# High halves of v and z by casting transfers of GpSimd, the half key tile as two 64-row products, and the logits of two half tiles in one pass

## The chip, the core and the metric

The program runs on one core of a Trainium2 chip. Time is the device time of one execution in microseconds (us). Five engines work side by side, each through its own list of instructions in order: TensorE (PE: matmul; PEld: the loading of its weights), VectorE (DVE), ScalarE (ACT), GpSimd (POOL), and SyncE (SP), which here only issues transfers between the chip's memory and the core. A granted clock of 1.00 in the profile is TensorE at 2.4 GHz.

## The reference, cut to what matters

Attention without a softmax over eight batches, and then a mixture of experts whose input is the attention's output.

```python
# u, v: (8, 2496, 256); z: (8, 2496, 64)
scores = scale * np.matmul(z, z.transpose(0, 2, 1))      # scale = 1 / 2496
attn = np.maximum(scores, 0.0) ** 2
x = u * np.matmul(attn, v)
logits = x @ w_gate                                       # (19968, 8)
# tokens are handed out to 8 experts, best logit first, 2496 to each
out[mask] = np.maximum(x[mask] @ w1[e], 0.0) @ w2[e]      # for each expert e
```

## The kernel before

A product in full precision is made of three in TensorE's faster number format (F32R): an operand a is split into a high part h = a rounded to that format and a low part l = a - h, and a.b is h.h + h.l + l.h. Most of the work beside TensorE is this splitting: a copy with a cast makes h, a subtraction makes l.

**Tiles.** A batch has 2496 tokens: 19 key tiles of 128 and a half one of 64, so KT = 20 with NT = 19 the number of the half one. Queries come in NQ = 5 groups, four of 512 columns and group 4 of 448. The program walks `seq`, 8 x 5 x 20 = 800 steps (b, g, kt). In step n, `av(n)` multiplies v's key tile kt with the squared scores r of that tile and adds to two accumulators acc0 and acc1 (the two halves of the 256 columns of v). A whole key tile takes six products of 128 rows.

**The half key tile.** v's 64 rows and z's 64 columns stand twice in their tiles, in rows 0 to 63 and 64 to 127. In r both halves are the same then. `split_lo` puts the low part into rows 64 to 127 of the high tile itself, so that one product of 128 rows gives h + l; `av` needs only four products (lines 1006 and 1009, for d = 0 and 1).

**Scores.** z has 64 channels, so score products have 64 rows; they stand in pairs, one on rows 0 to 63 and one on 64 to 127. `scores` makes 20 key tiles (GO = KT) in one burst of 60 products, at the start of each group, right behind the half key tile of the last group: it makes the key tiles 4 to 19 of the group that begins and 0 to 3 of the next. `rectify` takes them from one of six buffers (SCB) by ScalarE, and numbers 3, 6, 9 and 12 of a burst by VectorE (ASIDE).

**Splitting.** `square` (ScalarE), `split_hi` and `split_lo` (VectorE, line 993) run LA = 4 steps ahead of `av`, with five buffers of each. `split_hi` is ScalarE's (line 982) but for every second tile of group 4 (line 984, VectorE). z and v of batch b are loaded and split during group 4 of batch b - 1: `split_v` at step n0 - 20 + kt, `split_z` every fourth step (n0 is the batch's first step): on ScalarE for the high part (lines 935 and 943), on VectorE for the low part (936, 944). v's tiles turn in a ring of 22 buffers.

**The rest of VectorE.** At the end of a group it transposes the accumulators (`turn_acc`, line 1015) and multiplies with u (`times_u`, 1021); SP writes x out and reads it back as XS with tokens in partitions (`put_x`), and `post_logits` (line 1045) makes one column of logits of one tile: 32 passes for each group, 8 of them in group 4 on a tile of 64 rows. `logits_at` says at which steps they stand: `own` of them in the next group, `go` right behind the burst after that, `late` in the steps that follow it.

From step 20 on the program's order is the order on PE, ACT and DVE (`manual_schedule`); GpSimd and SP take their transfers in an order that the scheduler makes. Lines 748, 652 to 654, 590 and 781 belong to the expert part, which starts behind attention at about 1375 us; lines 590 and 781 are GpSimd's indirect gathers and scatters.

## Time and profile before

| | |
|---|---|
| time before, median of 3 runs | 2465.4 us (2464.53 to 2467.0) |
| the profiled execution, its own time | 2466.28 us |
| its span, first to last instruction | 2464.5 us |
| mean granted clock of TensorE | 0.996 |
| busy: PE, DVE, ACT, POOL | 98%, 84%, 62%, 15% of the span |
| largest groups of instructions: PE lines 1006, 1009, 1008 | 621.0, 615.9, 586.8 us |

A row of the timeline has the start in us, the time taken in us, engine, line, operation, the tile written and the tiles read, partitions x elements, the count, and in brackets the idle time of the engine before it with what ended it. Products are pipelined: one that "takes" 0.39 is followed by the next 0.23 later, so the pace is read from the starts. Instructions of one form that follow each other are merged into a row.

### The profile page before, as it was taken

To read this page: it belongs to the slowest core of one execution; us is meant where nothing else is said; L and a number is where in the kernel's file an instruction comes from. 1 tells how busy PE (TensorE), PEld (TensorE's weight loads), DVE (VectorE), ACT (ScalarE), POOL (GpSimd) and SP (SyncE) were. 2 spreads that over 40 slices of the span, in tenths; PEclk is the share of its full clock that TensorE was granted. 3 is DMA by queue.
4 is the path that set the end of the run, shared out by engine and by line. 5 is a ranking of instruction groups with operands and counts; after the bars stand their busy time and mean duration, and the time that the engine had idled before them with its cause. 6 is when DMAs were issued, how large, how long until landed. Compare 5 with 4: busy or idle time off the path is not lost.

```text
span 2464.5 us, 42329 instructions
## 1 busy us (share of the span) xinstructions
PE 2416.7 (98%) x14948; PEld 2016.6 (82%) x14948; DVE 2067.0 (84%) x6309; ACT 1535.1 (62%) x2986; POOL 362.5 (15%) x508
## 2 busy tenths in 40 slices
PE   8999999999999999999999899999999999999997
PEld 6888888888888888888887787788888888888886
DVE  7899898998999998989989897879796969696332
ACT  7898888898898988888987123333333333343332
POOL 3000000000000000000000022233242433333332
PEclk9999999999999999999999999999999999999999
DMA  4132131131131321312211022121212111122111
GB/s 150 34 105 62 52 114 30 53 110 52 45 109 37 100 66 52 114 27 55 76 52 43 9 70 69 34 73 47 70 51 69 44 64 54 45 86 68 43 42 34
DMA packets 156852, 154.86 MB, mean 63 GB/s; under 512 B 89440, under 2 KB 129888, under 8 KB 156512
## 3 DMA queue, kind: packets, MB, share of 16 engines
q1 hardware_dynamic: 141408, 110.72, 15.1%
q0 software_dynamic: 15232, 41.44, 5.3%
q8 instruction: 117, 1.92, 0.3%
q14 instruction: 95, 0.78, 0.1%
HBM read 111.22 MB, written 40.89 MB: 62 GB/s over the span
## 4 chain that ended last, share of the span: by engine, by line
PE 86%; DVE 8%; issue 3%; ACT 1%; DMA 1%; POOL 1%; POOLq 0%; ACTq 0%; DVEq 0%; SPq 0%
PE acc L1006 14%; PE acc L1009 14%; PE acc L1008 13%; PE sc L961 10%; PE y L748 10%; PE hp L652 5%; PE hp L653 5%; PE y L750 5%; PE hp L654 5%; PE srch L281 1%; DVE lo L993 1%; PE srch L529 1%; DVE vl L944 1%; DVE mask L124 1%; DVE lt L1045 1%
## 5 line engine op out<-in xcount | busy, mean ns | idle before, releaser
L1006 PE MATMUL acc<-hi,vh 128*128 128x512 f32 (+1 forms) x1600 | 621.0, 388 | 2.8 <-DVE hi L984 2.7
L1009 PE MATMUL acc<-hi,vl 128*128 128x512 f32 (+1 forms) x1600 | 615.9, 385 | 0.0
L1008 PE MATMUL acc<-lo,vh 128*128 128x512 f32 (+1 forms) x1520 | 586.8, 386 | 0.2 <-DVE lo L993 0.2
L993 DVE TENSOR_TENSOR lo<-r,hi 128x512 fp32r<-128x512 f32 (+1 forms) x760 | 510.5, 674 | 55.9 <-ACT hi L982 50.2
L730 ACT ACTIVATE hh<-hp 128x512 fp32r<-128x512 f32 (+1 forms) x319 | 187.2, 587 | 592.1 <-PE hp L654 474.1
L982 ACT ACTIVATE hi<-r 128x512 fp32r<-128x512 f32 (+1 forms) x701 | 454.3, 648 | 112.6 <-ACT r L977 65.0
L977 ACT ACTIVATE r<-r 128x512 f32<-128x512 f32 (+1 forms) x800 | 505.5, 643 | 2.7 <-DVE r L971 2.5
L1045 DVE SCALAR_TENSOR_TENSOR lt<-xs,wgb 128x256 bf16<-128x256 f32 x1248 | 473.4, 419 | 1.9
L748 PE MATMUL y<-w,hh 128*128 128x512 f32 x1216 | 447.7, 400 | 2.2 <-DVE y L773 1.4
L1006 PEld LDWEIGHTS acc<-hi,vh 128*128 128x128 f32 x1600 | 300.8, 188 | 72.9 <-issue 14.5
L973 ACT ACTIVATE r<-sc 128x512 f32<-128x512 f32 (+1 forms) x638 | 314.0, 614 | 53.5 <-PE sc L961 52.5
L1009 PEld LDWEIGHTS acc<-hi,vl 128*128 128x128 f32 x1600 | 300.8, 188 | 55.1 <-DVE vl L944 0.2
L1008 PEld LDWEIGHTS acc<-lo,vh 128*128 128x128 f32 x1520 | 285.8, 188 | 56.0 <-DVE lo L993 5.0
L748 PEld LDWEIGHTS y<-w,hh 128*128 128x128 f32 x1216 | 228.3, 188 | 51.7 <-DVE y L773 2.6
L652 PE MATMUL hp<-xh,w1h 128*128 128x512 f32 (+2 forms) x642 | 256.7, 400 | 2.1 <-DVE hl__30375 L732 1.3
L590 POOL DMA_INDIRECT xg<-xd,idx x160 | 176.7, 1104 | 540.4 <-issue 244.7
L961 PE MATMUL sc<-z,z 64*128 64x512 f32 (+1 forms) x1920 | 243.6, 393 | 8.9 <-DVE r L971 5.8
L653 PE MATMUL hp<-xl,w1h 128*128 128x512 f32 (+2 forms) x642 | 251.1, 391 | 0.1
L654 PE MATMUL hp<-xh,w1l 128*128 128x512 f32 (+2 forms) x642 | 249.0, 388 | 0.0
L961 PEld LDWEIGHTS sc<-z,z 64*128 64x128 f32 x1920 | 197.3, 185 | 48.5 <-issue 11.7
L256 POOL IOTA slot<- 128x256 bf16 x1 | 1.5, 1531 | 1346.4 <-DVE nrem L366 1346.4
L781 POOL DMA_INDIRECT out_dram<-y,idx x160 | 163.5, 1022 | 195.8 <-DVE y L773 111.6
(1180 smaller groups left out, 3173.6 us busy)
## 6 DMA issues: line engine op xcount, KB each, us to landing
ur<-in_u_dram SPq DMA_DIRECT2D x39, 512.0 KB, 3.9
vr<-in_v_dram SPq DMA_DIRECT2D x32, 512.0 KB, 3.9
xd<-tr SPq DMA_DIRECT2D x128, 128.0 KB, 2.3
xs<-xd SPq DMA_DIRECT2D x32, 512.0 KB, 4.5
wr<-in_moe_w_dram SPq DMA_DIRECT2D x32, 512.0 KB, 4.9
zr<-in_z_dram SPq DMA_DIRECT2D x40, 256.0 KB, 3.0
xd<-tr SPq DMA_DIRECT2D x28, 112.0 KB, 2.1
vr<-in_v_dram SPq DMA_DIRECT2D x8, 384.0 KB, 3.4
```

What stands on the lines that cost most here:

```text
L652: nc.tensor.matmul(p[:, c], wh, xh, start=(d == 0), stop=False)
L653: nc.tensor.matmul(p[:, c], wh, xl, start=False, stop=False)
L654: latest["mm"] = nc.tensor.matmul(p[:, c], wl, xh, start=False, stop=(d == DH - 1))
L748: nc.tensor.matmul(o, h[:, c], w.rearrange("p s d -> p (s d)"), start=(f == 0), stop=(f == FT - 1), skip_group_check=True)
L961: nc.tensor.matmul(pair[s], key[b, p][r, c * 128:c * 128 + 128], query[b, g][r, :w], start=key is ZH and query is ZH, stop=key is ZL)
L977: nc.scalar.activation(R[n], R[n], AF.Square)
L982: nc.scalar.activation(h, R[n], AF.Copy)
L993: recent["l"] = nc.vector.tensor_sub(l, a, h.bitcast(F32))
L1006: nc.tensor.matmul(o, vh, h, start=(kt == 0), stop=False)
L1008: nc.tensor.matmul(o, vh, l, start=False, stop=False)
L1009: nc.tensor.matmul(o, vl, h, start=False, stop=last)
L1045: nc.vector.scalar_tensor_tensor(t[r], XS[b, g][r, i], 1.0, WG["rows"][r, e], op0=OP.mult, op1=OP.mult, accum_out=lg[r, j, e:e + 1])
```

## The change

- `split_z` and `split_v` for all batches but the first have no copy by ScalarE: GpSimd's queue loads the high part straight from memory, with the cast in the transfer, into the tile zh or vh. The low parts are functions of their own, `low_z` and `low_v`, four steps later; the loads of z and v that they subtract from move with them (z from m - 8 to m - 2, v from 4g - 8 to 4g - 4).
- `split_hi` is ScalarE's for every tile from step 20 on, those of group 4 too.
- For the half key tile `split_lo` writes a low tile like the others, and `av` makes three pairs of 64-row products: rows 0 to 63 for d = 0 and rows 64 to 127 for d = 1.
- The half tiles of two batches share a tile TAIL, an even batch in rows 0 to 63 and an odd one in 64 to 127; the odd one's passes make the logits of both. `logits_at` gets other numbers.

```diff
@@ def split_z, split_v
-            src = ZI.pop((b, g))
-            return (nc.scalar.activation(ZH[b, g], src, AF.Copy),
-                    nc.vector.tensor_sub(ZL[b, g], src, ZH[b, g].bitcast(F32)))
+            if b:
+                nc.gpsimd.dma_start(ZH[b, g], z[b, :, 512 * g:512 * g + 512])
+                return
+            return nc.scalar.activation(ZH[b, g], ZI[b, g], AF.Copy), low_z(b, g)
+
+        def low_z(b, g):
+            return nc.vector.tensor_sub(ZL[b, g], ZI.pop((b, g)), ZH[b, g].bitcast(F32))
 
         def split_v(b, kt):
-            src = VR[b, kt // 4][:, kt % 4]
-            h = vp.tile([128, D], F32R, name="vh")
-            l = vp.tile([128, D], F32R, name="vl")
-            with in_turn(b):
-                nc.scalar.activation(h, src, AF.Copy)
-                nc.vector.tensor_sub(l, src, h.bitcast(F32))
-            VH[b, kt], VL[b, kt] = h, l
+            VH[b, kt] = vp.tile([128, D], F32R, name="vh")
+            if b == 0:
+                with in_turn(b):
+                    nc.scalar.activation(VH[b, kt], VR[b, kt // 4][:, kt % 4], AF.Copy)
+                    low_v(b, kt)
+            elif kt < NT:
+                nc.gpsimd.dma_start(VH[b, kt], v[b, 128 * kt:128 * kt + 128])
+            else:
+                for c in range(2):
+                    nc.gpsimd.dma_start(VH[b, kt][c * TL:(c + 1) * TL], v[b, 128 * kt:])
+
+        def low_v(b, kt):
+            VL[b, kt] = vp.tile([128, D], F32R, name="vl")
+            nc.vector.tensor_sub(VL[b, kt], VR[b, kt // 4][:, kt % 4], VH[b, kt].bitcast(F32))
@@ def split_hi, split_lo
-            if n >= KT and (seq[n][1] != NQ - 1 or n % 2 or n == B * NQ * KT - 2):
+            if n >= KT:
                 nc.scalar.activation(h, R[n], AF.Copy)
...
-            if seq[n][2] == NT:
-                nc.vector.tensor_sub(h[TL:], a[TL:], h[TL:].bitcast(F32))
-                return
-            l = wk.tile([128, 512], F32R, name="lo", bufs=LA + 1)[:, :width(seq[n][1])]
-            recent["l"] = nc.vector.tensor_sub(l, a, h.bitcast(F32))
-            LO[n] = l
+            LO[n] = wk.tile([128, 512], F32R, name="lo", bufs=LA + 1)[:, :width(seq[n][1])]
+            recent["l"] = nc.vector.tensor_sub(LO[n], a, h.bitcast(F32))
@@ def av
-            last = kt == NT
-            h, l = HI.pop(n), LO.pop(n, None)
-            for d in range(2):
-                o = ACC[b, g][d][:, :width(g)]
-                c = slice(d * 128, (d + 1) * 128)
-                vh, vl = VH[b, kt][:, c], VL[b, kt][:, c]
-                nc.tensor.matmul(o, vh, h, start=(kt == 0), stop=False)
-                if not last:
-                    nc.tensor.matmul(o, vh, l, start=False, stop=False)
-                nc.tensor.matmul(o, vl, h, start=False, stop=last)
+            o = [ACC[b, g][d][:, :width(g)] for d in range(2)]
+            c = [slice(d * 128, (d + 1) * 128) for d in range(2)]
+            h, l, vh, vl = HI.pop(n), LO.pop(n), VH[b, kt], VL[b, kt]
+            parts = ((vh, h), (vh, l), (vl, h))
+            if kt < NT:
+                for d in range(2):
+                    for i, (w, x) in enumerate(parts):
+                        nc.tensor.matmul(o[d], w[:, c[d]], x, start=(kt == 0 and i == 0), stop=False)
+                return
+            for i, (w, x) in enumerate(parts):
+                for d in range(2):
+                    r = slice(d * TL, (d + 1) * TL)
+                    nc.tensor.matmul(o[d], w[r, c[d]], x[r], start=False, stop=(i == 2))
@@ def put_x, post_logits
+                if b % 2 == 0:
+                    TAIL[b // 2] = wk.tile([128, D], F32, name="tail", bufs=1)
                 r = TL * (b % 2)
-                nc.sync.dma_start(XS[b, g][r:r + TL, n], xd[lo + 128 * n:lo + w])
+                nc.sync.dma_start(TAIL[b // 2][r:r + TL], xd[lo + 128 * n:lo + w])
...
-                r = slice(TL, 128) if b % 2 else slice(0, TL)
-                j = B * NT + b // 2
+                r, src, j = slice(0, 128 if b % 2 else TL), TAIL[b // 2], B * NT + b // 2
@@ def logits_at
-            own, go, late = ((11, 12, 9), (16, 12, 4), (20, 10, 2), (0, 14, 18), (6, 14, 12))[n % NQ]
+            own, go, late = ((8, 14, 10), (14, 12, 6), (22, 10, 0), (0, 14, 18), (4, 14, 14))[g]
             if n == B * NQ - 3:
-                own, go, late = 20, 12, 0
+                own, go = 20, 12
+            if g == NQ - 1 and b % 2 == 0 and b + 2 < B:
+                own, go, late = 4, 12, 8
@@ the plan of a batch
-                    at(m - 8, load_z, b, g)
+                    at(m - 2, load_z, b, g)
                     at(m + 1, split_z, b, g)
-                    at(n0 - KT + 4 * g - 8, load_v, b, g)
+                    at(m + 5, low_z, b, g)
+                    at(n0 - KT + 4 * g - 4, load_v, b, g)
                 for kt in range(KT):
                     at(n0 - KT + kt, split_v, b, kt)
+                    at(n0 - KT + kt + 4, low_v, b, kt)
```

How the order moves, at three places. On TensorE at the end of group 1 of batch 3, where the score burst of group 2 follows; before (acc_7353 and acc_7354 are the two accumulators, z_... the z tiles):

```order
L1009 MATMUL acc_7354<-hi,vl 128x512
L1006 MATMUL acc_7353<-hi,vh 128x512
L1009 MATMUL acc_7353<-hi,vl 128x512
L1006 MATMUL acc_7354<-hi,vh 128x512
L1009 MATMUL acc_7354<-hi,vl 128x512
L961 MATMUL sc<-z_6532,z_6465 128x512 x12
```

and after:

```order
L1014 MATMUL acc_7383<-hi,vl 128x512
L1019 MATMUL acc_7382<-hi,vh 128x512
L1019 MATMUL acc_7383<-hi,vh 128x512
L1019 MATMUL acc_7382<-lo,vh 128x512
L1019 MATMUL acc_7383<-lo,vh 128x512
L1019 MATMUL acc_7382<-hi,vl 128x512
L1019 MATMUL acc_7383<-hi,vl 128x512
L972 MATMUL sc<-z_6549,z_6488 128x512 x12
```

Four products of 128 rows have become six of 64 rows, alternating between the accumulators; the score products still follow at once.

On VectorE from the last steps of group 4 of batch 2 to the first ones of batch 3, across the burst at 522.14 us (r<-sc are the four rectifications, lt the logits); before:

```order
L944 TENSOR_TENSOR vl<-vr,vh 128x256
L971 TENSOR_SCALAR r<-sc 128x512 x4
L1021 TENSOR_TENSOR tr<-tr,ur 128x512
L1021 TENSOR_TENSOR tr<-tr,ur 128x384
L1045 SCALAR_TENSOR_TENSOR lt,lg<-xs,wgb 128x256 x14
L993 TENSOR_TENSOR lo<-r,hi 128x512
L1045 SCALAR_TENSOR_TENSOR lt,lg<-xs,wgb 128x256 x2
L993 TENSOR_TENSOR lo<-r,hi 128x512
L1045 SCALAR_TENSOR_TENSOR lt,lg<-xs,wgb 128x256 x2
L993 TENSOR_TENSOR lo<-r,hi 128x512
```

and after:

```order
L956 TENSOR_TENSOR vl<-vr,vh 128x256
L982 TENSOR_SCALAR r<-sc 128x512 x4
L1031 TENSOR_TENSOR tr<-tr,ur 128x512
L1031 TENSOR_TENSOR tr<-tr,ur 128x384
L1055 SCALAR_TENSOR_TENSOR lt,lg<-xs,wgb 128x256 x14
L1001 TENSOR_TENSOR lo<-r,hi 128x512
L956 TENSOR_TENSOR vl<-vr,vh 128x256
L1055 SCALAR_TENSOR_TENSOR lt,lg<-xs,wgb 128x256 x2
L1001 TENSOR_TENSOR lo<-r,hi 128x512
L956 TENSOR_TENSOR vl<-vr,vh 128x256
L1055 SCALAR_TENSOR_TENSOR lt,lg<-xs,wgb 128x256 x2
L1001 TENSOR_TENSOR lo<-r,hi 128x512
```

The vl ahead of the rectifications is that of key tile 15 now and was that of 19; four subtractions of vl stand among the first steps of the new batch.

On GpSimd, whose list had no transfer during attention, this stands for batch 4, after the change (z_10651 is the first z tile of batch 5, one batch ahead; the next four are those of batch 4):

```order
L949 DMA vh<-in_v_dram 128x256 x2
L935 DMA z_10651<-in_z_dram 128x512
L935 DMA z_8700<-in_z_dram 128x512
L935 DMA z_8761<-in_z_dram 128x512
L935 DMA z_8828<-in_z_dram 128x512
L935 DMA z_8897<-in_z_dram 128x512
L949 DMA vh<-in_v_dram 128x256 x17
L952 DMA vh<-in_v_dram 64x256 x2
```

26 transfers for a batch have come in; the z tile of batch 1 stands ahead of them all, near the start of the program.

## Rows read from the trace of the kernel before

**Rows 1.** Waits of TensorE, 165 to 1330 us: total us, times, longest.
```profile
PE sc L961 <- DVE r L971: 5.3, 7, 0.8
```
**Rows 2.** Timeline of TensorE, end of a group and its normal burst.
```profile
590.70 0.39 PE L1009 MATMUL acc<-hi,vl 128*128 128x512 f32 x1
...
591.61 0.39 PE L1009 MATMUL acc<-hi,vl 128*128 128x512 f32 x1
591.92 1.66 PE L961 MATMUL sc<-z,z 64*128 64x512 f32 x12
...
599.18 0.50 PE L1006 MATMUL acc<-hi,vh 128*128 128x512 f32 x1
```
**Rows 3.** Timeline of TensorE, the burst at the start of batch 3.
```profile
522.14 4.08 PE L961 MATMUL sc<-z,z 64*128 64x512 f32 x30
526.97 3.79 PE L961 MATMUL sc<-z,z 64*128 64x512 f32 x30 [0.74 <-DVE r L971]
530.68 0.50 PE L1006 MATMUL acc<-hi,vh 128*128 128x512 f32 x1
```
**Rows 4.** Timeline of VectorE, ahead of and in the same burst.
```profile
519.00 0.39 DVE L984 CAST hi<-r 128x448 fp32r<-128x448 f32 x1
...
525.93 0.38 DVE L944 TENSOR_TENSOR vl<-vr,vh 128x256 fp32r<-128x256 f32 x1
526.24 1.88 DVE L971 TENSOR_SCALAR r<-sc 128x512 f32<-128x512 f32 x3
```
**Rows 5.** Timeline of VectorE, the normal burst of rows 2.
```profile
593.68 0.66 DVE L971 TENSOR_SCALAR r<-sc 128x512 f32<-128x512 f32 x1
```
**Rows 6.** Stretches, group 4: us; busy PE, PEld, DVE, ACT, POOL; clock; DMA; GB/s.
```profile
490.80:522.10 31.30, 31.30 (x179) 27.61 (x178) 30.14 (x82) 30.35 (x71) 0.00 (x0) 1.00 0.44 135
```
**Rows 7.** Waits of VectorE in that stretch, 490.8 to 522.1 us.
```profile
DVE r L971 <- PE sc L961: 0.7, 2, 0.4
```
**Rows 8.** Timeline of TensorE, products of 448 columns: batch 2, last batch.
```profile
497.60 0.47 PE L1006 MATMUL acc<-hi,vh 128*128 128x448 f32 x1
...
1357.41 0.36 PE L1006 MATMUL acc<-hi,vh 128*128 128x448 f32 x1
...
1371.40 0.36 PE L1006 MATMUL acc<-hi,vh 128*128 128x448 f32 x1
```
**Rows 9.** Groups of instructions by form: busy us, mean ns of one, idle before.
```profile
L982 ACT ACTIVATE hi<-r 128x448 fp32r<-128x448 f32 x81 | 49.0, 605 | 33.2 <-issue 24.8 <-PE acc L1009 5.4 <-ACT r L977 2.9
...
L943 ACT ACTIVATE vh<-vr 128x256 fp32r<-128x256 f32 x160 | 70.9, 447 | 0.0
```
**Rows 10.** Timeline of GpSimd, gathers one behind the other.
```profile
1733.74 0.96 POOL L590 DMA_INDIRECT xg<-xd,idx  x1 [0.30 <-issue]
1735.01 0.95 POOL L590 DMA_INDIRECT xg<-xd,idx  x1 [0.30 <-issue]
```
**Rows 11.** Timeline of GpSimd and TensorE, a gather and what waited for it.
```profile
1432.66 1.43 POOL L590 DMA_INDIRECT xg<-xd,idx  x1 [0.31 <-issue]
...
1435.97 0.44 PE L684 MATMUL y<-identf,xg 128*128 128x128 f32 x2 [0.45 <-DMA xg<-xd,idx]
```
**Rows 12.** Transfers issued: count, KB each, median us to landing.
```profile
vr<-in_v_dram SPq DMA_DIRECT2D x32, 512.0 KB, 3.9
```
**Rows 13.** Timeline of VectorE and TensorE, key tile 8 of batch 3, group 0.
```profile
540.35 0.68 DVE L993 TENSOR_TENSOR lo<-r,hi 128x512 fp32r<-128x512 f32 x1
...
541.95 0.39 PE L1008 MATMUL acc<-lo,vh 128*128 128x512 f32 x1
```
**Rows 14.** Timeline of TensorE at the start.
```profile
7.36 0.79 PE L961 MATMUL sc<-z,z 64*128 64x512 f32 x2 [1.76 <-ACT z L935]
```
**Rows 15.** Stretches at the start, columns as in rows 6.
```profile
6.00:8.00 2.00, 0.64 (x4) 0.54 (x6) 0.66 (x2) 0.63 (x1) 1.24 (x14) 1.00 1.07 359
```
**Rows 16.** Timeline of TensorE, last group of attention.
```profile
1352.26 0.47 PE L1006 MATMUL acc<-hi,vh 128*128 128x448 f32 x1 [2.68 <-DVE hi L984]
```
**Rows 17.** Timeline of VectorE at that place.
```profile
1351.82 0.39 DVE L984 CAST hi<-r 128x448 fp32r<-128x448 f32 x1
```

14 lines of the change are left out of this document (7 added, 7 removed).

## The prediction, made before the changed kernel ran

> **What bounds the kernel now.** I read the waits of TensorE first, then its timeline at the ends of the query groups, then VectorE at the same places. Between 165 and 1330 us TensorE waits for nothing but a VectorE result, 5.3 us in seven waits [rows 1]; all the rest of attention is its own issue rate. So an edit there is worth either matmul time that goes away or one of the few stalls. Three of those can be seen.
>
> First the normal end of a group: a product of 512 columns every 0.2275 us ((591.61 - 590.70)/4), a gap of 0.31 instead of that at the change to the 64-row score products, then 60 of them in 7.26 us (591.92 to 599.18) [rows 2]. They run in pairs, so a pair costs at most 7.26/30 = 0.242.
>
> Second, the score burst at the start of a batch, after group 4: 8.54 us (522.14 to 530.68) for the same 60 products, with a wait for VectorE in the middle [rows 3]. That is 1.28 more than in [rows 2], and there are seven such bursts (the seven waits of [rows 1]). The reason is in VectorE's rows: its first rectification comes 4.10 us after the burst's start (526.24), in the normal burst 1.76 after (593.68 against 591.92) [rows 2 to 5]. Had it begun at 524.96, 1.28 earlier and 2.82 after the start, TensorE would have lost nothing. It is late because group 4 of every batch but the last carries the splitting of the next batch's v and z: VectorE is busy 30.14 of 31.30 us and ScalarE 30.35 [rows 6], and VectorE waits only 0.7 us in the whole stretch [rows 7].
>
> Third, within that group TensorE takes 24.54 us (497.60 to 522.14 [rows 3, 8]) for 118 products of 448 columns. The same form without v and z beside it takes (1371.40 - 1357.41)/69 = 0.2028 each [rows 8], 23.93 for 118; with 0.2 for the way in and out some 0.4 per batch is lost to operands that come just in time.
>
> **The half key tile.** Before, four 128-row products for each group; now three pairs of 64-row products. Before: 4 x 0.2275 = 0.910. After: three pairs at 0.242 or less. The 7.26 of the burst hold its own way in and out (the first product behind it took 0.50 instead of 0.39 [rows 2]), so I take 0.235 a pair, 0.705 in all, and a gain of 0.20; the ends are 0.184 (0.242 a pair) and 0.2275 (a pair as cheap as one product). In the order the six stand right ahead of the score products, which have the same 64-row form, so the gap of 0.31 only moves from behind them to ahead of them. 32 groups x 0.20 and seven groups of 448 columns x 0.175 give **-7.6** (7.0 to 8.7). The fortieth tail is followed by 128-row products and VectorE work that ends later; it counts zero.
>
> What the Trainium skill says against this stands in "TensorEngine Tiling (Array Packing)", Key Properties: a change of the tiling mode drains TensorE. The gap of 0.31 in [rows 2] agrees that a change costs something. By that rule the price depends on the neighbours: with tails that are a region of their own, 39 more changes would be paid; this is a rival below.
>
> **High parts by casting transfers.** ScalarE loses 140 copies of vh at 447 ns [rows 9] and 35 of z; it gains the 79 casts of group 4 that VectorE had, at 605 ns [rows 9]. In one group 4 that is -20 x 0.447 and +10 x 0.605, so ScalarE falls by 2.9 or more from 30.35; the 0.95 us that it has free cover it already, and no wait of TensorE in [rows 1] is for ScalarE. VectorE loses ten casts of 0.39 [rows 4] ahead of each of the seven bursts, and since the low parts come four steps later, four subtractions of 0.31 (525.93 to 526.24 [rows 4]) move behind the burst: 3.9 + 1.2 = 5.1 us less, where 1.28 less was wanted. So the stall goes, **-9.0** (7 x 1.28; 0 if something else keeps VectorE late), and so should the 0.4 of just-in-time operands, **-2.8** (0 to -2.9).
>
> Late next is the subtraction of the low part itself, which now waits for GpSimd's transfer, with every later lo of VectorE queued behind it. Rows of a casting transfer there are none. The nearest are GpSimd's indirect gathers of the same 128 rows of 1 KB: 1.27 us from one to the next [rows 10], 3.3 us from the start to the consumer that waited for it (1432.66 to 1435.97 [rows 11]). A buffer of the ring of 22 comes free when TensorE is through with step kt-2 of group 4, steps of 6 x 0.2028 = 1.22 us. So 14 transfers (kt 2 to 15) fall behind by 13 x 0.05 = 0.7, and the last one asked for, six steps (7.3 us) ahead of the burst, has landed 7.3 - 3.3 - 0.7 = 3.3 us before the burst begins; it is read after the burst has begun. The four transfers of z stand in GpSimd's queue while TensorE does the burst before. So I take **0**. The spare time is 3.3 and the 2.82 of above, less some 1 for the transposes ahead: 5 us, or 0.4 on each of 13 intervals. Up to 1.7 us a transfer costs nothing; beyond it TensorE waits. From below, a transfer cheaper than a gather gains nothing either. SP's queue loses nothing: the source tiles are asked for 8 steps (9.8 us) ahead and land in 3.9 [rows 12]; before it was the same 8 steps for v.
>
> The four subtractions that moved are now among the first steps of group 0, where VectorE also does two logits a step. At key tile 8 of it a lo ends at 541.03 (540.35 + 0.68) and is used at 541.95 [rows 13]: 0.92 to spare. Four times 0.31 take 1.24, so TensorE waits 0.32 in each of seven batches: **+2.2** (0, if the lead is rebuilt by the burst that is no longer late, to 4.2 at the 0.38 that one takes).
>
> At the start the casting transfer of batch 1's first z tile is now queued beside the first loads. TensorE's second score pair waits for such a load (1.76 us, through ScalarE), while the queues already run at 359 GB/s [rows 14, 15]; 256 KB at that rate are **+0.7** (0 to 1.5, twice, if it is ahead of two loads).
>
> **Logits and the last group.** 24 of 56 half-tile passes go; in groups 0 to 3 VectorE does not hold TensorE up [rows 1], and the burst of group 2 gets 14 passes behind it instead of 12, as that of group 1 has already without a wait: 0. In the last group TensorE waits 2.68 us for a cast of VectorE behind its logits [rows 16, 17]. The cast goes to ScalarE, the lo behind it comes only by the cast's own 0.4 earlier: **-0.4** (0 to -2). The expert part has the same instructions as before: 0.
>
> Sum: -7.6 - 9.0 - 2.8 + 2.2 + 0.7 - 0.4 = **-16.9 us**. The profiled execution took 2466.28, 0.9 over the median of 2465.4; 2465.4 - 16.9 = **2448.5**.
>
> **Rivals.**
> - *The stall stays*: VectorE is held in group 4 by something else, a low part that waits 1 to 2 us for its transfer, or ScalarE's extra casts. Then the 9.0 and 2.8 do not come and the late start hides no 2.2: -7.6 + 0.7 - 0.4 + 2.2 = -5.1, **2460.3**. For it: VectorE's 96% and the new wait; against it, 5.1 us of relief.
> - *GpSimd's queue is the bound*, the case on the other side: at 2.0 us a transfer TensorE loses 13 x (2.0 - 1.7) = 3.9 in each batch, 27 in seven, **2476**. It decides from 16.9/(7 x 13) = 0.19 over 1.7, so 1.9 us a transfer. For it: 26 transfers in the 38 us from one batch's burst before group 4 to the next, and no row that shows what a casting one costs to issue; against it, the gather's 1.27.
> - *Each tail pays a change of form of its own*, as the rule of the Trainium skill would have it if tails and scores counted as different modes. By rows: 0.31 - 0.2275 = 0.08 in and 0.11 out (0.50 - 0.39) [rows 2], 39 x 0.19 = 7.4; **2455.9**. Against it: both have the form 64 rows by 128 columns.
> - *The pairs do not overlap*, so the change does not do what it says: six products at 0.2275 are 1.365 instead of 0.910, +17.7 in place of -7.6, **2473.8**. Against it: the score products, 0.242 a pair.
>
> **How the numbers follow.** Forecast 0.70, stall stays 0.11, GpSimd 0.10, own change of form 0.05, no overlap 0.04. The range goes from 2443 (every bound of the forecast on its good side: -8.7 - 9.0 - 2.9 - 2 = -22.6) to 2461, which takes in the change of form and the stall that stays, and leaves out GpSimd, no overlap and little else: 2 in 10. About 0.2% (4.9 us, 2460.5) is what a measurement tells from no change. Faster: forecast, change of form, and half of the case at 2460.3: 0.80. Slower: GpSimd beyond 2.0 and no overlap: 0.12. Same: 0.08.
>
> **What would show it.** Right: the seven bursts at the start of a batch take 7.3 us and the wait for the rectification is gone from TensorE's list; three pairs ahead of each burst in about 0.7; group 4 in some 24.0 with the tail; small waits for lo near key tile 8 of group 0; GpSimd's issues 1.2 to 1.3 us apart. Wrong: VectorE's subtraction of vl released by a transfer for microseconds at a time; GpSimd busy without a gap through group 4; a tail of more than 0.9; or a burst of group 0 that still takes 8.5.

## The result and the profile after

The changed kernel took **2441.4 us** (median of 4; 2439.4 to 2443.0) against 2465.1 for the kernel before: ratio 0.9901 (95%: 0.9886 to 0.9916), 23.7 us less. 2448.5 were forecast, with 2443 to 2461 as the range. Two further sets of runs on other chips gave 0.9913 (0.9896 to 0.9929) and 0.9919 (0.9905 to 0.9932), 22.0 and 20.8 us less. So the direction was right and the size too small. The first set lies 1.6 us under that range; at the distances of the two others the kernel would lie inside it, near its lower end. The profiled execution of the changed kernel took 2443.0, its span is 2441.0.

What the prediction spoke of within attention is there. The waits of TensorE from 165 to 1330 us, where [rows 1] had 5.3 us in seven, are an empty list. Its timeline at the start of batch 3 (start, us, then the instruction) is this:

```profile
515.96 0.36 PE L1014 MATMUL acc<-hi,vl 128*128 128x448 f32 x1
516.26 0.47 PE L1019 MATMUL acc<-hi,vh 64*128 64x448 f32 x2
516.56 0.38 PE L1019 MATMUL acc<-lo,vh 64*128 64x448 f32 x2
516.76 0.38 PE L1019 MATMUL acc<-hi,vl 64*128 64x448 f32 x2
516.97 7.31 PE L972 MATMUL sc<-z,z 64*128 64x512 f32 x60
524.21 0.50 PE L1014 MATMUL acc<-hi,vh 128*128 128x512 f32 x1
```

Against [rows 3] the 60 score products take 7.24 us (516.97 to 524.21) instead of 8.54, in one piece. The three pairs of the tail take 0.71 (516.26 to 516.97). The gap of 0.30 is ahead of them (515.96 to 516.26) and none is left behind. In a normal group of 512 columns the tail takes 0.80, and group and burst together are 0.20 shorter, as forecast:

```profile
584.83 0.50 PE L1019 MATMUL acc<-hi,vh 64*128 64x512 f32 x2
...
585.63 1.55 PE L972 MATMUL sc<-z,z 64*128 64x512 f32 x12
```

VectorE is at its first rectification 2.16 us after the burst's start (519.13 here, 4.10 in [rows 4]), and only one low part still stands in front of it:

```profile
517.13 0.69 DVE L1001 TENSOR_TENSOR lo<-r,hi 128x512 fp32r<-128x512 f32 x1
517.73 1.17 DVE L1025 STREAM_TRANSPOSE tr<-acc 128x448 f32<-128x448 f32 x2
518.83 0.38 DVE L956 TENSOR_TENSOR vl<-vr,vh 128x256 fp32r<-128x256 f32 x1
519.13 1.49 DVE L982 TENSOR_SCALAR r<-sc 128x512 f32<-128x512 f32 x2
```

The stretch of group 4, in the columns of [rows 6], and VectorE's waits in it, as [rows 7]:

```profile
486.20:516.90 30.70, 30.70 (x182) 27.68 (x180) 27.43 (x69) 27.69 (x56) 12.61 (x24) 1.00 0.87 229
```

```profile
DVE lo L1001 <- ACT hi L993: 2.1, 8, 0.3
DVE r L982 <- PE sc L972: 1.1, 3, 0.4
```

VectorE is busy 27.43 of 30.70 us and waits for no transfer. GpSimd's timeline shows casting transfers 1.21 us apart, each 0.53 long and released by TensorE: the buffer paces it, its queue has 0.69 to spare at each.

```profile
494.54 0.53 POOL L949 DMA_DIRECT2D vh<-in_v_dram  x1 [2.08 <-PE acc L1014]
495.75 0.53 POOL L949 DMA_DIRECT2D vh<-in_v_dram  x1 [0.69 <-PE acc L1014]
496.96 0.53 POOL L949 DMA_DIRECT2D vh<-in_v_dram  x1 [0.69 <-PE acc L1014]
```

**Where the time went.** I cut the two profiled executions (spans 2464.5 and 2441.0) at the same places:

| part of the span | before | after | difference | predicted |
|---|---|---|---|---|
| to the last group's score burst | 1339.0 | 1322.6 | -16.4 | -16.5 |
| that burst to the last product of attention | 34.2 | 32.0 | -2.2 | -0.4 |
| from there to the first product on gathered tokens | 61.0 | 59.6 | -1.4 | 0 |
| from there to the end of GpSimd's last instruction | 1020.85 | 1020.52 | -0.3 | 0 |
| from there to the end of the span | 9.45 | 6.36 | -3.1 | 0 |

The first line holds within 0.1, in part by chance (see the part on why the prediction came out low). What the sum missed lies behind the last score burst. The table's last line is read from GpSimd's last row and the span, here of the kernel before and of the changed one: 2464.5 - 2454.08 - 0.97 = 9.45, and 2441.0 - 2433.70 - 0.97 = 6.33, or 6.36 before rounding.

```profile
core 0 of [0], span 2464.5 us
...
2454.08 0.97 POOL L781 DMA_INDIRECT out_dram<-y,idx  x1 [0.31 <-issue]
```

```profile
core 0 of [0], span 2441.0 us
...
2433.70 0.97 POOL L781 DMA_INDIRECT out_dram<-y,idx  x1 [0.30 <-issue]
```

In that time GpSimd alone still has an instruction open, the closing wait of the program (10.85 us before, 7.68 after, counted from its own start); all other engines stand behind it. The profile shows no transfer in it from 1.1 us behind GpSimd's last instruction on: the share of the DMA engines is 0.00 from 2456.2 to 2463.0 us before and from 2435.8 to 2440.0 after. So it is not data still on the way that makes the difference.

### The profile page after: what moved, and what is told of

It reads as the page before. It is cut to its first block, busy times and chain, and to the rows that moved or that the text cites. A ratio compares the mean times of both kernels' runs of the same rounds, so it can differ in the third digit from the quotient of the medians.

```text
span 2441.0 us, 42804 instructions
## 1 busy us (share of the span) xinstructions
PE 2403.2 (98%) x15028; PEld 2012.3 (82%) x15028; DVE 2028.3 (83%) x6182; ACT 1522.4 (62%) x2890; POOL 458.9 (19%) x690
## 5 line engine op out<-in xcount | busy, mean ns | idle before, releaser
L1001 DVE TENSOR_TENSOR lo<-r,hi 128x512 fp32r<-128x512 f32 (+1 forms) x800 | 536.0, 673 | 82.0 <-ACT hi L993 79.0
L1014 PE MATMUL acc<-hi,vh 128*128 128x512 f32 (+1 forms) x1520 | 589.8, 388 | 0.2 <-ACT vh L946 0.2
L1014 PE MATMUL acc<-hi,vl 128*128 128x512 f32 (+1 forms) x1520 | 584.7, 385 | 0.0
L993 ACT ACTIVATE hi<-r 128x512 fp32r<-128x512 f32 (+1 forms) x780 | 500.3, 642 | 119.2 <-ACT r L988 86.3
L1055 DVE SCALAR_TENSOR_TENSOR lt<-xs,wgb 128x256 bf16<-128x256 f32 x1192 | 449.1, 417 | 0.0
L1014 PEld LDWEIGHTS acc<-hi,vh 128*128 128x128 f32 x1520 | 285.4, 188 | 66.8 <-issue 13.8
L1014 PEld LDWEIGHTS acc<-hi,vl 128*128 128x128 f32 x1520 | 285.5, 188 | 51.9
L972 PE MATMUL sc<-z,z 64*128 64x512 f32 (+1 forms) x1920 | 236.8, 389 | 4.3 <-ACT z L937 2.7
L935 POOL DMA_DIRECT2D z<-in_z_dram x35 | 18.7, 534 | 960.0 <-DVE lt L1055 530.0
```

The source lines that it names most:

```text
L972: nc.tensor.matmul(pair[s], key[b, p][r, c * 128:c * 128 + 128], query[b, g][r, :w], start=key is ZH and query is ZH, stop=key is ZL)
L993: nc.scalar.activation(h, R[n], AF.Copy)
L1001: recent["l"] = nc.vector.tensor_sub(LO[n], a, h.bitcast(F32))
L1014: nc.tensor.matmul(o[d], w[:, c[d]], x, start=(kt == 0 and i == 0), stop=False)
L1055: nc.vector.scalar_tensor_tensor(t[r], src[r], 1.0, WG["rows"][r, e], op0=OP.mult, op1=OP.mult, accum_out=lg[r, j, e:e + 1])
```

## The experiments

Five columns are read from each run's profile. *Stretch*: from the first product of group 4 to the first product of the next batch's group 0, so group 4 with the burst behind it, mean of seven. *Group 0*: its products, mean of seven. *Last burst*: where the score burst of the last group starts. *To experts*: from there to the first product on gathered tokens. *End*: from GpSimd's last instruction to the end of the span. Times against the kernel before are differences of medians on the same chip; the other columns come from one profile each.

| run | against before | ratio, 95% | stretch | group 0 | last burst | to experts | end |
|---|---|---|---|---|---|---|---|
| before | | | 33.08 | 26.99 | 1339.0 | 95.2 | 9.45 |
| changed | -23.7 | 0.9886-0.9916 | 31.22 | 27.40 | 1322.6 | 91.5 | 6.36 |
| e1_tails | -5.9 | 0.9967-0.9986 | 33.43 | 26.89 | 1333.1 | 95.7 | 9.46 |
| e2_casts | -10.5 | 0.9943-0.9971 | 31.57 | 27.52 | 1331.7 | 93.9 | 6.36 |
| e3_no_casts | -9.7 | 0.9947-0.9975 | 32.78 | 26.89 | 1328.8 | 96.3 | 9.46 |
| g4_logits | -5.6 | 0.9968-0.9987 | 32.36 | 26.99 | 1334.1 | 95.2 | 9.46 |
| e4_hi_dve | -15.7 | 0.9925-0.9958 | 31.55 | 27.40 | 1324.6 | 94.7 | 6.36 |
| e7_low2 | -17.7 | 0.9910-0.9943 | 32.89 | 26.91 | 1331.0 | 91.7 | 6.36 |
| g3_last_dve | -17.6 | 0.9912-0.9946 | 31.22 | 27.40 | 1322.3 | 94.6 | 6.36 |
| e6_spare | -1.5 | 0.9984-1.0004 | 33.10 | 26.99 | 1340.9 | 95.9 | 6.93 |
| h4_one | +0.8 | 0.9994-1.0013 | 33.1 | 26.99 | 1340.1 | 95.2 | 9.54 |
| f1_after | -22.0 | 0.9896-0.9929 | 31.30 | 27.38 | 1322.3 | 93.0 | 6.36 |
| h1_after | -20.8 | 0.9905-0.9932 | 31.21 | 27.41 | 1323.4 | 91.5 | 6.36 |
| e8_premask | -19.9 | 0.9906-0.9939 | 32.2 | 26.91 | 1325.5 | 90.9 | 6.36 |
| g1_premask | -22.7 | 0.9891-0.9924 | 31.2 | 27.40 | 1322.3 | 91.1 | 6.36 |
| g2_spread | -25.5 | 0.9881-0.9914 | 31.22 | 26.89 | 1319.2 | 90.9 | 6.36 |
| h2_spread_only | -25.2 | 0.9883-0.9913 | 31.23 | 26.89 | 1319.5 | 91.6 | 6.36 |
| h3_both | -27.4 | 0.9875-0.9905 | 31.22 | 26.89 | 1318.6 | 91.2 | 6.36 |

### The tails alone, and all but the tails

e1_tails is the kernel before with the six half-height products in `av` (and the full low part of the tail in `split_lo`) taken from the change; e2_casts is the changed kernel with these two functions as before.

```diff
-            if seq[n][2] == NT:
-                nc.vector.tensor_sub(h[TL:], a[TL:], h[TL:].bitcast(F32))
-                return
...
+            for i, (w, x) in enumerate(parts):
+                for d in range(2):
+                    r = slice(d * TL, (d + 1) * TL)
+                    nc.tensor.matmul(o[d], w[r, c[d]], x[r], start=False, stop=(i == 2))
```

> The kernel before with the paired half key tile alone. Theory (the terms of the prediction hold, and what came beyond them lies behind the last score burst): 32 tails x 0.20 + 7 x 0.175 = 7.6 us off, 2457.5 in the attention, the seven late bursts of 8.5 us and their wait for a rectification stay. If the wait of GpSimd at the end of the program (10.9 us before, 7.7 after the change) follows the transfers that GpSimd issues, it stays 10.9 here. Rival (the end of the program and the clock there differ from one execution to the next, whatever the kernel): the end may be 7.7 here as well, 2454.5. Rival (the tail brings less or more than 0.20): a normal burst with its tail does not go from 7.25 to 7.15 and the part of the group before it not from 26.99 to 26.89.

> The changed kernel with the half key tile as before (four products of 128 rows), so the casting transfers and the logits of two half tiles alone. Theory: 7.6 us over the changed kernel, 2449.0; the seven bursts take 7.3 us, no wait for a rectification; the end of the program with GpSimd's last wait at 7.7 as in the changed kernel, if that follows the transfers that GpSimd issues. Rival (execution to execution): the end is anywhere between 7.7 and 10.9, 2449 to 2452.

e1 gave -5.9, not -7.6. The tail itself is as forecast: group 0 goes from 26.99 to 26.89 and the burst behind it from 7.25 to 7.14, 0.2 together. But the stretch gets longer by 0.35, because its burst now waits more. Waits of TensorE in e1, 165 to 1330 us, where [rows 1] has 5.3:

```profile
PE sc L961 <- DVE r L971: 10.9, 7, 1.6
```

TensorE comes to the burst 0.11 us sooner (24.43 us after the group's start instead of 24.54), and the burst takes 9.00 instead of 8.54. So seven tails of group 4 bring nothing while that stall stands. That the wait grows by more than the tail gives is measured; why is not shown. e2 lost 9.1 us up to the last burst against the changed kernel, not 7.6. Three of its seven groups 4 ran in a slower rhythm (last section), 3 x 0.46 = 1.4; the rest, 7.7, is the forecast size. e2's gain in the time, 10.5 and not the 16 expected, misses by that 1.4 and by 2.4 on the way to the experts (93.9 against 91.5), where its profile has the fall of the clock that is shown under the last group; some 2 stay unexplained.

### The casts away, and two logits passes moved

e3_no_casts has the high parts copied by ScalarE, with loads, low parts and the casts of group 4 where they were before. g4_logits is the kernel before with one number row changed, so that two passes of VectorE leave group 4 for group 3 ahead of it (in `logits_at`, the three numbers of group 2). The changed kernel has the same three numbers there.

```diff
...
-                nc.gpsimd.dma_start(VH[b, kt], v[b, 128 * kt:128 * kt + 128])
...
+                nc.scalar.activation(VH[b, kt], VR[b, kt // 4][:, kt % 4], AF.Copy)
...
```

```diff
-            own, go, late = ((11, 12, 9), (16, 12, 4), (20, 10, 2), (0, 14, 18), (6, 14, 12))[n % NQ]
+            own, go, late = ((11, 12, 9), (16, 12, 4), (22, 10, 0), (0, 14, 18), (6, 14, 12))[n % NQ]
```

> The changed kernel with the high parts of v and z copied by ScalarE, and the loads, low parts and the casts of group 4 where they were before: left of the change are the paired tails and the logits of two half tiles. Theory: as the tails alone, 2457.5, and up to 3 us less if the unpredicted gain behind the last score burst comes of the logits; the seven late bursts stay at 8.5. GpSimd's wait at the end is 10.9 if it follows the transfers. Rival (the logits, not the casts, cured the late bursts): the bursts take 7.3 and the time is near 2448.

> The kernel before with one row of numbers changed: the two logits of group 2 that it leaves for group 4... that is, those that follow group 3's burst, are done within group 3, (22, 10, 0) for (20, 10, 2). Theory (the 0.4 lost in group 4 of each batch, a gap of 0.25 at its eleventh key tile and smaller ones behind, comes of logits passes between VectorE's splitting, not of the copies and casts): group 4 without the gaps, 24.1 instead of 24.53 (or 24.57 where the slower rhythm of its products holds), and the burst behind it no longer than 8.55, so 0.4 to 1.0 a batch, 3 to 7 us under the kernel before. Rival (the gaps are of ScalarE's copies and VectorE's casts, as the prediction had it): they stay, and the time is that of before.

g4 rests on what VectorE does in the kernel before at the one large gap of group 4. Timeline of VectorE, then of TensorE, kernel before:

```profile
508.78 0.42 DVE L1045 SCALAR_TENSOR_TENSOR lt<-xs,wgb 128x256 bf16<-128x256 f32 x1
509.12 0.08 DVE L1045 DVE_READ_ACCUMULATOR lt<-xs,wgb 128x1 f32 x1
509.12 0.39 DVE L984 CAST hi<-r 128x448 fp32r<-128x448 f32 x1
509.54 0.63 DVE L993 TENSOR_TENSOR lo<-r,hi 128x448 fp32r<-128x448 f32 x1
```

```profile
509.87 0.37 PE L1006 MATMUL acc<-hi,vh 128*128 128x448 f32 x1
510.22 0.48 PE L1008 MATMUL acc<-lo,vh 128*128 128x448 f32 x1
510.54 0.37 PE L1009 MATMUL acc<-hi,vl 128*128 128x448 f32 x1
```

A logits pass of 0.34 stands ahead of the low part, which ends at 510.17 (509.54 + 0.63); its product starts at 510.22, and TensorE loses 0.27 there (0.35 from 509.87 and 0.32 from 510.22 instead of 0.20 each). With the two passes gone, in e3 as in g4, no such gap is left, although ScalarE and VectorE still do all their copies and casts. In g4 group 4 is no shorter for it (24.58 instead of 24.54), since all seven ran in the slower rhythm of the last section. But the list of TensorE's waits from 165 to 1330 is empty and the bursts take 7.78 instead of 8.54: one row of numbers removes 0.72 of a stretch, 5.0 us in seven, and 5.6 in the time. So part of what the prediction put down to the casting transfers belongs to the logits table, for which it had put down 0. e3, with tails and logits, is 10.2 ahead at the last burst, close to the 10.8 that e1's 5.9 and g4's 4.9 make; the bursts of 8.3 to 8.8 and TensorE's wait in them (7.4 us in seven, 1.3 at most) stay, as expected. The time agrees with that, 9.7 less.

### VectorE's casts back, and the low parts sooner

e4_hi_dve is the changed kernel with every second cast of group 4 on VectorE again.

```diff
-            if n >= KT:
+            if n >= KT and (seq[n][1] != NQ - 1 or n % 2 or n == B * NQ * KT - 2):
```

> The changed kernel with every second cast of group 4 on VectorE again, as before; the high parts of v and z still come by GpSimd's casting transfers. Theory (VectorE's relief ends the late burst): ten casts of 0.39 stand ahead of each burst again, VectorE rises by 3.9 us from 27.4 in a stretch of 30.7; four low parts are still behind the burst (1.2 us), so the rectification comes about as late as the 1.28 less 1.2: bursts of 7.2 to 7.6, 2441.4 to 2444. Rival (the casts of VectorE are what holds it up, the later low parts count little): bursts of 8.5 again, 2441.4 + 7 x 1.3 = 2450.5. Second rival (copies and casts of VectorE keep GpSimd from issuing its transfers, as the Trainium skill has it in 'SBUF - State Buffer'): GpSimd's issues are no longer 1.2 apart, low parts of v wait for transfers, and the time goes over 2451.

The stretch of group 4 in e4:

```profile
486.60:517.40 30.80, 30.80 (x184) 27.79 (x182) 30.06 (x78) 23.85 (x48) 12.95 (x24) 1.00 0.85 223
```

VectorE is as busy as in [rows 6] (30.06 us), yet the bursts take 7.1 to 7.4. So its load was not the cause. What is left is what stands ahead of the rectification in its queue: four low parts of v and the logits passes of group 2 are gone from there, here as in the changed kernel. Four of the seven groups 4 ran in the slower rhythm, 4 x 0.45 = 1.8 of the 2.0 that e4 is later at the last burst. GpSimd's issues stay 1.21 apart. Its timeline, and the casts of VectorE at the same places:

```profile
507.10 0.61 POOL L949 DMA_DIRECT2D vh<-in_v_dram  x1 [0.69 <-PE acc L1014]
508.31 0.53 POOL L949 DMA_DIRECT2D vh<-in_v_dram  x1 [0.60 <-PE acc L1014]
...
511.96 0.69 POOL L949 DMA_DIRECT2D vh<-in_v_dram  x1 [0.69 <-DVE z L940]
```

```profile
507.20 0.39 DVE L995 CAST hi<-r 128x448 fp32r<-128x448 f32 x1
...
512.15 0.39 DVE L995 CAST hi<-r 128x448 fp32r<-128x448 f32 x1
```

The Trainium skill ("SBUF — State Buffer", Who interferes with whom) says that a cast of VectorE can take the port pair that GpSimd writes descriptors through, and that GpSimd then stands still. The trace agrees in part. In seven of the nine places of this profile where a cast lies wholly inside an issue, the issue takes 0.61 to 0.71 instead of 0.53; in the changed kernel, without the casts, no single issue in group 4 is that long. That is less than the cast's own 0.39, and the 0.69 that the queue has to spare takes it up: the next issue starts in time. e4's time is 15.7 under the kernel before, not 21 to 24. Besides those 2.0, 3.2 of that are on the way to the experts (94.7 against 91.5), which g3 takes up.

e7_low2 is the changed kernel with v's low parts two steps behind their transfer instead of four.

```diff
-                    at(n0 - KT + kt + 4, low_v, b, kt)
+                    at(n0 - KT + kt + 2, low_v, b, kt)
```

> The changed kernel with the low parts of v taken two steps after their transfer instead of four. Theory (the 0.5 us that TensorE loses in group 0 of each batch, with 55 ns left to a low part at key tiles 7 and 8, comes of the subtractions moved behind the burst): two of four come back ahead of it, so 0.4 to 0.5 in each of seven batches goes, 2438 where the changed kernel takes 2441.4; the transfers land 2.0 to 2.4 us after issue, less than two steps (2.43), so VectorE waits for none by more than 0.2. Rival (the transfer is late for two steps): VectorE's subtraction of vl is released by a transfer, the rectification comes late, and the time is 2441 to 2450.

e7 went the other way: 4.3 us over the changed kernel on its chip. Group 0 did come down to 26.91, but bursts of 8.0 to 10.8 are back. VectorE's waits from 165 to 1330 us, and its timeline ahead of the worst one, with TensorE's row behind it:

```profile
DVE vl L956 <- DMA vh<-in_v_dram: 17.6, 22, 2.9
```

```profile
347.61 0.42 DVE L956 TENSOR_TENSOR vl<-vr,vh 128x256 fp32r<-128x256 f32 x1 [0.81 <-DMA vh<-in_v_dram]
...
350.25 0.42 DVE L956 TENSOR_TENSOR vl<-vr,vh 128x256 fp32r<-128x256 f32 x1 [0.74 <-DMA vh<-in_v_dram]
```

```profile
355.80 0.50 PE L972 MATMUL sc<-z,z 64*128 64x512 f32 x2 [1.75 <-DVE r L982]
```

The premise of the expectation was wrong: most transfers of v land later than 2.0 to 2.4 us after their issue. Their row in the list of transfers (count, KB, median us from issue to landing), in the second profile of the changed kernel (f1_after) and in e7:

```profile
vh<-in_v_dram POOLq DMA_DIRECT2D x133, 128.0 KB, 4.5
```

```profile
vh<-in_v_dram POOLq DMA_DIRECT2D x133, 128.0 KB, 4.9
```

Two steps, 2.4 us, are not enough for that, and what VectorE waits for a transfer is handed to TensorE's burst (8.3 us in seven waits from 165 to 1330 us, 5.3 in the kernel before). This is the mechanism of the rival "the stall stays"; with four steps, 4.9 us, VectorE waits for none of them from 165 to 1330 us in the first profile of the changed kernel, and once, 0.2 us, in the second. So the short burst is not to be had with low parts ahead of it that wait, nor, with the paired tails, by the logits passes alone (e3: 8.3 to 8.8). The ten casts were not needed (e4). Whether the later low parts would do it alone, without the moved logits passes or without the 6.5 us by which ScalarE is relieved in the stretch (23.85 for 30.35), was not run.

### The last group

> The changed kernel with every second cast of the last group alone on VectorE again, as before; all that precedes is as in the changed kernel. Theory (what the last group and the way into the expert part gained beyond the 0.4 predicted is the casts that VectorE no longer does there): from the last score burst to the first expert product some 95.0 to 95.7 us, as before, where the changed kernel has 91.2 to 92.7; the time 2 to 3 over the changed kernel, 19 to 21 under the kernel before. Rival (the gain there is the logits of two half tiles or chance of the clock): 91.2 to 92.7 here too, 22 to 23.7 under the kernel before.

Its edit is e4's rule for the last group alone. To the last burst it is the changed kernel (1322.3); from there it needs 94.6 against 91.5 to 93.0, and the time is 3 to 6 us over the changed kernel's distances. So the casts that VectorE no longer does in the last group are worth 1.6 to 3.1 us there. The smaller figure is against f1_after, whose clock falls at the same place as g3's (below); the larger ones hold that fall as well. The wait that the prediction looked at hardly shows it. Waits of TensorE, 1325 to 1395 us, kernel before and changed one:

```profile
PE acc L1006 <- DVE hi L984: 2.7, 1, 2.7
PE sc L1071 <- DVE xt L1058: 1.6, 1, 1.6
```

```profile
PE acc L1014 <- DVE lo L1001: 2.7, 1, 2.7
PE y L298 <- DVE lg L1087: 1.2, 1, 1.2
...
PE sc L1081 <- DVE xt L1068: 0.2, 1, 0.2
```

The long wait is as long as before. It is the next one, for the last transposes (`xt`), that falls from 1.6 to 0.2 (g3: 1.2). The other part is the clock. In [rows 16] the wait is followed by a granted clock of 0.66 over the next microseconds, which is a mean: part of the 5 us at the level of 1.2 GHz, the rest at 2.4; in the first profile of the changed kernel the same wait is followed by 1.00, in the second one by 0.66 (rows in this order):

```profile
1353.00:1358.00 5.00, 5.00 (x17) 4.52 (x18) 4.93 (x16) 1.51 (x3) 0.00 (x0) 0.66 0.00 0
```

```profile
1336.00:1341.00 5.00, 5.00 (x26) 4.63 (x27) 5.00 (x19) 3.31 (x7) 0.00 (x0) 1.00 0.13 46
```

```profile
1336.00:1341.00 5.00, 5.00 (x19) 4.47 (x18) 5.00 (x19) 2.21 (x5) 0.00 (x0) 0.66 0.07 25
```

The last two executions differ by 33.5 - 32.0 = 1.5 us in the last group, so 1.5 of the first profile's gain comes in some executions only. The third profile of the changed kernel (h1_after) is like the first, 1.00 and 32.0; that of g3 has 0.66 in these 5 us. Between executions with the fall, the way to the experts is 2.2 shorter than before (95.2 and 93.0). What decides on the fall was not tried.

### The end of the program

> The kernel before, with 182 small plain transfers more that GpSimd issues in group 4 of each batch but the last (26 each, 128 rows of 256 bytes into a tile that nobody reads). Theory (the wait of GpSimd at the end of the program follows from its having issued direct transfers): that wait is 7.7 instead of 10.9 and the time 3 us less, 2463 where the kernel before takes 2466, as the transfers themselves cost nothing (4 us at most if they slow the queue of the loads). Rival (the wait at the end is shorter for another reason: the later loads, or what ScalarE and VectorE no longer do): it stays at 10.9 and the time is that of before or a little over.

> The kernel before with one small plain transfer of GpSimd more, at the start of group 4 of the first batch (128 rows of 256 bytes into a tile that nobody reads). Theory A (GpSimd's wait at the end is shorter as soon as it has issued one direct transfer): 7.7 to 8.2 instead of 10.85, the time 3 us under the kernel before. Theory B (it depends on how many transfers GpSimd has issued in all, where they stand in its queue's ring): it stays at 10.8 or takes a value of its own, and the time is that of before.

```diff
+        def spare(b, i):
+            t = wk.tile([128, 64], F32, name="spare", bufs=2)
+            nc.gpsimd.dma_start(t, v[b, 64 * i:64 * i + 128, :64])
...
+                for i in range(26):
+                    at(n0 - KT + i * KT // 26, spare, b, i)
```

With 182 of these transfers, on the kernel before, the end is 6.93 us (2458.8 - 2450.86 - 0.97 = 6.97 with rounded numbers); with a single one 9.54 (2464.9 - 2454.42 - 0.97 = 9.51). Last row of GpSimd in e6 and in h4:

```profile
2450.86 0.97 POOL L781 DMA_INDIRECT out_dram<-y,idx  x1 [0.30 <-issue]
```

```profile
2454.42 0.97 POOL L781 DMA_INDIRECT out_dram<-y,idx  x1 [0.30 <-issue]
```

In all 18 profiles the end is 6.36 with the 182 casting transfers, 6.93 with 182 plain ones, and 9.45 to 9.54 with one or none. That many direct transfers of GpSimd shorten the end is shown; one is not enough; what it is in their number or place that counts stays open. e6 as a whole came to -1.5 only, which its interval (0.9984 to 1.0004) does not tell from no change, since its last burst is 1.9 later, 1.6 of it already at the start of batch 1 (184.4 against 182.8).

### What repeats, and a better version

> The changed kernel a second time, on the chip of the other runs of this call and with a profile of its own: which parts of its time repeat. Theory: the attention up to the last score burst repeats within 0.5 us (bursts of 7.2, group 4 in 24.0, the burst of the last group at 1322.6), and GpSimd's last wait is 7.7 again; the last group and the expert part, where the granted clock falls for 3.4 to 10 us in one place or another, differ from the first profile by up to 4 us. Rival: all of it repeats, the last group without a fall of the clock too, so the 2.3 us that the last group gained belongs to the change.

> The changed kernel once more, as the one that the next two runs are compared with on the same chip. Theory (16.4 us up to the last score burst and 3.1 at the end of the program are the change's on every chip, the last group and the way into the expert part bring 2 to 4 more): 21.5 to 24 us under the kernel before.

Up to the last burst the changed kernel repeats within 1.1 us (1322.3 to 1323.4; 0.5 was expected), the end exactly. What differs is the last group (the clock, above) and the expert part with the same instructions. So the change is worth 21 to 24 us (h1's 20.8 is under the 21.5 expected), of which 15.6 to 16.7 and 3.1 are in known places.

The other runs of this part change VectorE's order further: e8_premask is e7 with the premask moved, g1_premask the changed kernel with it, g2_spread that with the logits spread as well; h2_spread_only and h3_both are the changed kernel with the spread and with both.

> The same with the low parts two steps after the transfer, and the premask of the expert choice, which VectorE does for all batches at the start of the last group, moved for all but the last batch to group 3 of the batch after. Theory (the 2.7 us for which TensorE waits in the last group is VectorE's, behind logits and premask): the wait goes to 0.5 or less, 2.2 us under the run with the low parts alone, 2436; and if the fall of the clock behind that wait comes of it, 1 to 2 more. Rival (the wait is of something else, the logits of batch 7 or the transposes): it stays at 2.7 and the time is that of the other.

> The changed kernel, low parts four steps after their transfer as there, with only the premask moved from the start of the last group to group 3 of each following batch. Theory (the 2.7 us of waiting in the last group is VectorE's, behind logits and premask, and the clock falls behind it in some executions): 2.3 to 3 us under the changed kernel, so 24.5 to 26 under the kernel before; the seven bursts stay at 7.2. Rival (the premask in group 3 costs what it saves): as the changed kernel, 22 to 23.7 under the kernel before.

> The same, and the eighteen logits that follow group 3 of each batch spread over 15 steps of group 0 instead of 10. Theory (the 0.4 to 0.5 that TensorE loses in group 0 at key tiles 7 and 8 comes of two logits a step behind the four low parts): VectorE gains about half a pass of 0.35 in each of the first steps, group 0 goes from 27.4 to 26.9, seven times, so 3.3 us under the run with the premask alone, 28 to 29 under the kernel before. Rival (the loss only moves to a later key tile, since VectorE is busy without a gap to key tile 12): group 0 stays over 27.2 and the time within 1 us of the other.

> The changed kernel with the eighteen logits behind group 3 spread over 15 steps of group 0 instead of 10, the premask where it was. Theory (the 0.45 lost in group 0 of each batch goes, nothing else moves): 3.2 us under the changed kernel on the same chip. Rival (the time gained in front is lost in the last group, whose wait for VectorE stays at 2.7 us and behind which the clock may fall): 1.5 or less.

> The spread logits and the moved premask together. Theory (the wait of 2.7 us in the last group is gone, but the way from there into the expert part waits 1.8 for VectorE instead of 0.2, so that 0.5 to 2 are left): 0.5 to 2 us under the run with the spread alone, 3.7 to 5.2 under the changed kernel. Rival (what the last group gains, the expert part gives back whole): the time of the run with the spread alone.

```diff
-            first_in.setdefault((B * NQ - 1) * KT, []).append((premask, (c, c + 16)))
+            at((((c + 15) // NT + 1) * NQ + 3) * KT + 8 + c // 16 % 2, premask, c, c + 16)
```

```diff
+            over = 15 if g == 3 else 10
...
-                    + [m0 + KT + 1 + i * 10 // max(late, 1) for i in range(late)])
+                    + [m0 + KT + 1 + i * over // max(late, 1) for i in range(late)])
```

Spreading the logits does what it should: group 0 from 27.41 to 26.89 in all seven, 3.9 us at the last burst, and 4.3 in the time on the same chip (2445.8 to 2441.5, ranges apart); g2 is 2.9 under g1. The loss did not move to another key tile. The premask is less clear. g1 came to -22.7, not to the 24.5 to 26 expected: that is where its rival had it, at the changed kernel's distances. The move takes the wait of 2.7 away (0.5 is left in h3's list), and the last group goes from 32.0 to 29.8; but the wait for `xt` goes from 0.3 to 2.0, and the way to the experts is only 0.4 shorter (91.6 to 91.2). Waits of TensorE in h3, 1325 to 1395 us:

```profile
PE sc L1081 <- DVE xt L1068: 2.0, 1, 2.0
...
PE acc L1014 <- DVE lo L1001: 0.5, 1, 0.5
```

h3's median is 2.3 us under h2's, with overlapping ranges, but 0.9 of that is there before the last group begins (1319.5 and 1318.6). e8's median is 2.3 under e7's as well, but its profile is 5.5 us ahead at the last burst already, where TensorE's waits in the seven bursts differ (4.8 us in all against 8.3). So a gain by the premask beyond 0.4 is not shown. **h3_both beats both kernels**: 2439.2 on a chip where the kernel before takes 2466.6 and the changed one 2445.8; its runs (2437.9 to 2441.3) lie under all of the changed kernel's (2445.3 to 2447.1).

## Why the prediction came out low

**What bounds the kernel now**: right. Removing stalls of VectorE and matmul time moved the last burst by 16.4 us where 16.5 were put down. That the two agree within 0.1 is in part luck, since terms of it miss in both directions: the new wait in group 0 cost 1.4 more, and in each of the seven batches the burst ahead of group 3 gave 0.15 beyond a tail's share (7.27 us before, 7.00 after; 6.99 with the tails alone), 1.1 in all.

**The half key tile**, -7.6: right in size (0.20 a group, 7.7 in e2). The premise that it adds to the other terms holds only with the stall gone; alone it gave 5.9. The rival of a change of form for each tail falls. The Trainium skill's drain at a mode change ("TensorEngine Tiling (Array Packing)", Key Properties) fits the 0.30 ahead of a tail, but there is only one for tail and scores together: none stands between 516.76 and 516.97.

**The late burst and the operands of group 4**, -9.0 and -2.8: right in sum. The stretch fell by 1.86, less 0.2 for its tail is 1.66, 11.6 in seven. The causes were put wrong, so that the sum came right in part by luck: of 5.1 us of relief 3.9 were given to the casts, and e4 needs none of them; the operands that came just in time were held up by logits passes, and moving these, which stands in the sum with 0, brings 5.0 us of stretch alone (g4).

**GpSimd's queue**, 0: right, with less to spare than was worked out. A casting transfer takes 4.5 us from issue to landing (the median of f1_after), not the 3.3 of a gather; the slack of four steps, 4.9 us, and the place of the last low parts behind the burst took that up. e7 shows two steps to be too few.

**The new wait in group 0**, +2.2: right in place, too small; 27.40 - 26.89 = 0.51, 3.6 in seven, because two key tiles lose and not one.

**The start**, +0.7: the first burst takes 8.7 instead of 7.8 us, and 8.3 to 9.4 in all kernels with these transfers against 7.4 to 8.5 in those with one or none. Right within that scatter.

**Logits and the last group**, -0.4: here the prediction failed first, with a term that was mis-sized. It counted one cast ahead of one wait. Six more of 0.4 us (1353.32 to 1367.04 us in the kernel before) no longer stand ahead of the last transposes, which cuts the next wait by 1.4, and a fall of the clock behind the long wait, 1.5 us, comes in some executions only. -2.2 to -3.7 were seen against 95.2 before.

**Expert part**, 0: this is the other step that failed. The instructions are the same, and yet 3.1 us are missing at its end. The sum had no term for the end of the program, for which nothing in the rows of before gave a reason. That GpSimd's direct transfers shorten it is shown (6.93 instead of 9.45 with 182 plain ones); by what mechanism stays open. With -3.1, and -2.2 to -3.7 instead of -0.4, the sum is -21.8 to -23.3, where the three sets of runs gave -20.8 to -23.7.

## What to carry to other kernels

A stall is better read from what stands in the engine's queue ahead of the instruction that is waited for than from how busy the engine is: 30.06 of 30.80 us busy cost 0.2 us a burst at most (7.14 to 7.43 in e4, 7.2 in the changed kernel) once the deferrable work stood behind the burst. A consumer of a transfer gets its slack in steps of the loop, and has to be moved together with it; two steps too few brought the stall back, larger than before. And a sum of terms should go on to the last instruction of the program: moving work between engines also changes what the last stage and the program's end wait for.

## What the hardware showed beyond that

The products of 448 columns in group 4 run in one of two rhythms at a granted clock of 1.00. Six take 1.24 us in g4 (500.72 to 501.96) and 1.22 in the changed kernel (499.75 to 500.97):

```profile
500.72 0.37 PE L1006 MATMUL acc<-hi,vh 128*128 128x448 f32 x1
...
501.96 0.37 PE L1006 MATMUL acc<-hi,vh 128*128 128x448 f32 x1
```

```profile
499.75 0.36 PE L1014 MATMUL acc<-hi,vh 128*128 128x448 f32 x1
...
500.97 0.36 PE L1014 MATMUL acc<-hi,vh 128*128 128x448 f32 x1
```

A group stays in the rhythm it entered, to its end or to the next pause (in h4_one six products take 1.24 up to the gap at the eleventh key tile and 1.22 from there), so a whole group without such a pause costs 24.02 or 24.46 with the same instructions, 24.11 or 24.57 with the old tail. The slow one held in all seven groups of g4, four each of e3 and e4, three of e2, one each of f1_after and e8 and none of the first profile of the changed kernel. What chooses it was not tried. The other surprise is the closing wait of GpSimd, 3.1 us shorter after many direct transfers.
